# Turning batch 1's attention output with TensorE instead of DMA transposes, in a sliding-window attention and hard-swish kernel

## The chip, the cores and the metric

The kernel runs on one core of one Trainium2 chip. The metric is the device time of one execution in microseconds (us). Before the change three runs gave 332.79, 333.71 and 334.29 us, so the median is 333.71 us. The execution that was profiled took 332.83 us, and its span, which the times in the views below count from, is 331.1 us.

## What is computed

Two stages follow each other. The first is causal attention with a window of 64 keys, for 8 batches of 8 heads, 576 tokens each, head size 64. The second is an up-projection, a hard-swish and a down-projection over all 8 * 576 = 4608 tokens of width 512.

```python
scores = scale * np.matmul(q, k.transpose(0, 1, 3, 2))
rel = pos[:, None] - pos[None, :]
scores = np.where((rel >= 0) & (rel < 64), scores, -1e9)
attn = softmax(scores)                       # over the keys
x = np.matmul(attn, v).transpose(0, 2, 1, 3).reshape(4608, 512)
h = x @ w_in                                 # 512 -> 2048
out = (h * np.clip(h + 3, 0, 6) / 6) @ w_out # 2048 -> 512
```

## The kernel before, in words

**Pairs and blocks.** Attention goes by pairs of heads: pair `t` is batch `t // 4`, heads `2g` and `2g + 1` with `g = t % 4`. So batch 1 is the pairs 4 to 7, and batch 2 begins with pair 8. The second stage goes by blocks of 512 tokens. It reads `xT`, the attention output with the 512 features on the partitions (four groups of 128, one for each `g`) and tokens along the row. Block 1 is tokens 512 to 1023: the end of batch 0 and most of batch 1. Its first matmuls can start only when the columns of batch 1 are in `xT`, group by group.

**Work of a pair.** `turn` (L267) turns its queries and keys with 36 small TensorE transposes into two PSUM tiles (`tk`, `tq`), `turned` (L280) copies them to SBUF, `s_first` and `s_rest` (L289, L299) make the scores, `weights` (L314) the masked exponentials. `pv` (L381) multiplies these by V: 48 small matmuls (L396) whose sums, with the row sums in extra columns, fill two PSUM banks, the tile `o`. `pv_out` (L401) runs on VectorE: one row-sum reduction (L405), a reciprocal (L407), and three multiplies that normalise and write `opg0` (the first 64 tokens, L410) and `opl` (the other 512, two instructions at L415) to SBUF. `opg0` and `opl` have two buffers each, so pair `t + 2` writes where pair `t` wrote.

**Two ways into `xT`.** `x_` (L422) issues DMA transposes from the SP queue (L429): for batch 1, one for `opl` and one for `opg0` of each pair. `x_turned` (L440) turns the same data with five TensorE transposes (L444, L446) into a PSUM tile `xp`, which ScalarE copies to `xT` (L450). Before the change pairs 4 and 5 go by `x_` and pairs 6 and 7 by `x_turned`.

**PSUM.** There are eight banks: `ps_o` has one buffer of two banks (the tile `o`, and now and then half of it for a second-stage tile), `ps_t` three single banks, `ps_h` two single banks (the tiles `tk` and `tq` of `turn`, and some second-stage tiles), `ps_acc` one (the down-projection's sums `acc`).

**Order.** The instructions of each engine run in the order of the program, and that is written out by hand. The second stage lies in a queue `moe` of units; `weave(n)` emits the next `n` of them. In the stretch around the change these are the down-projection units of block 0, each four matmuls of 512 columns (L503). Each four units end with a copy on ScalarE (L509) and a store from the SP queue (L511). Ten of the sixteen have been emitted when pair 4 begins its `pv`. After pair 7 come `turn_two(8)` (the turn and copies of pair 8), the rest of the units, `shift(2)` (two SP DMAs at L156 and L157 that copy V of batch 2 within SBUF to a second alignment, after the loads of that V), and `begin(1, ...)` (L536): the up-projections of block 1 (L475) for groups 0 to 2 of three tiles, then `x_turned(7)`, then a fourth tile, then group 3 of all four. From there `group` (L709) runs pair after pair with units of the second stage between them. The POOL queue holds the loads: q and k of batch 2, V of batch 2, q and k of batch 3 are issued before this stretch (L118, L136), V of batch 3 after it.

```python
    for t in range(n, n + 4):              # L765, n = 4: batch 1
        pv(t)
        pv_out(t)
        if t < n + 2:
            x_(t)
        weave(2 if t == n else 1)
    turn_two(2 * NG)
    x_turned(n + 2)
    weave(len(moe))
    shift(2)
    queue_block(1)
    begin(1, (ps_t, ps_t, ps_acc, ps_o), lambda: x_turned(n + 3))
```

## Time and profile before

| | |
|---|---|
| median of the runs (lowest to highest) | 333.71 us (332.79 to 334.29) |
| the profiled execution | 332.83 us, span 331.1 us |
| mean granted TensorE clock | 0.985 of full speed |
| TensorE matmul busy | 304.5 us, 92% of the span |
| TensorE weight loads busy | 155.4 us, 47% |
| ScalarE busy | 186.2 us, 56% |
| VectorE busy | 177.1 us, 53% |
| GpSimd (POOL) busy | 114.7 us, 35% |
| DMA transposes at L429 | 30 of `opl`, 26 of `opg0`; median 2.9 and 3.2 us from issue to landing |

In the views PE is TensorE's matmuls, PEld its weight loads, DVE VectorE, ACT ScalarE, POOL GpSimd, SP the engine that issues stores and DMA transposes. A line of a timeline gives the start, the time until its last instruction ends, the engine, the source line, the tile written and those read, the number of instructions and, in brackets, the engine's idle time before it and what ended that. Matmuls overlap, so the spacing of two starts says what a piece of work costs and the duration of one does not. The profile has the tile `opg0` under the name `opg` and the fourth up-projection tile under `hTo`.

### The profile page before, as it was taken

The page shows a single profiled execution, that of the slowest core. Times are in us where ns is not written, and L with a number is a line of the kernel's source. Part 1 is how long each engine was busy: PE and PEld are TensorE (multiplying, and loading weights), DVE is VectorE, ACT ScalarE, POOL GpSimd, SP SyncE. Part 2 cuts the span into 40 slices and gives each one's busy share as a digit, 9 for nine tenths or more (in the row PEclk, how much of TensorE's full clock was granted, in tenths as well). Part 3 has the DMA queues.
Part 4 walks back from the last instruction along what each step waited for, and adds up shares of the span by engine and source line. Part 5 has one row for each costly group of instructions (what it writes and reads, how often), then busy time and mean ns, then how long its engine had stood idle before and what let it go on. Part 6 is the DMA issues. An engine that isn't in the chain of part 4 may idle for free.

```text
span 331.1 us, 11063 instructions
## 1 busy us (share of the span) xinstructions
PE 304.5 (92%) x4769; PEld 155.4 (47%) x4812; DVE 177.1 (53%) x382; ACT 186.2 (56%) x347; POOL 114.7 (35%) x149
## 2 busy tenths in 40 slices
PE   6879978198999999999999999999999999999992
PEld 3643444144555555555555555555544444444440
DVE  8676655128845673666366636663665354434300
ACT  2857673049857674677467736773685255554320
POOL 8952340007665633563356335633333000000000
PEclk9999999789999999999999999999999999999998
DMA  7999999932744965596559546954111200011011
GB/s 96 163 210 207 205 205 212 189 100 22 93 132 92 177 74 146 96 162 80 147 106 150 90 138 115 170 79 122 52 52 52 81 2 32 32 40 58 33 66 69
DMA packets 58680, 35.97 MB, mean 109 GB/s; under 512 B 40960, under 2 KB 52736, under 8 KB 58624
## 3 DMA queue, kind: packets, MB, share of 16 engines
q0 software_dynamic: 35712, 18.81, 42.6%
q1 hardware_dynamic: 22912, 16.38, 19.3%
q8 instruction: 39, 0.64, 0.8%
q14 instruction: 17, 0.14, 0.1%
HBM read 37.62 MB, written 9.44 MB: 142 GB/s over the span
## 4 chain that ended last, share of the span: by engine, by line
PE 78%; issue 10%; POOL 5%; DVE 3%; DMA 2%; ACT 1%; POOLq 0%; DVEq 0%; ACTq 0%
PE acc L503 35%; PE hT L475 33%; PE o L396 4%; PE s L308 2%; PE tk L274 2%; DMA V<-in_v_dram 2%; POOL qk L107 1%; POOL Pz L329 1%; POOL V L126 1%; DVE gT L484 1%; PE tq L274 1%; DVE opg L362 1%; POOL V L136 1%; ACT xT L376 0%; POOL P L326 0%
## 5 line engine op out<-in xcount | busy, mean ns | idle before, releaser
L484 DVE SCALAR_TENSOR_TENSOR gT<-t,hT 128x512 bf16<-128x512 bf16 x142 | 96.9, 687 | 84.2 <-ACT t L483 83.6
L503 PE MATMUL acc<-wout,gT 128*128 128x512 bf16 x547 | 134.4, 381 | 3.3 <-issue 1.9
L475 PE MATMUL hT<-xT,win 128*128 128x512 bf16 x555 | 135.1, 379 | 2.3 <-DVE gT L484 1.0
L483 ACT ACTIVATE t<-hT,half_const 128x512 bf16<-128x512 f32 x142 | 96.9, 688 | 52.1 <-PE hT L475 50.4
L475 PEld LDWEIGHTS <-win 128*128 128x128 bf16 x576 | 55.3, 98 | 67.3 <-issue 3.0
L503 PEld LDWEIGHTS <-gT 128*128 128x128 bf16 x576 | 54.8, 98 | 64.4 <-issue 1.2
L326 POOL TENSOR_TENSOR P<-e,first 64x256 bf16<-64x256 bf16 x24 | 15.9, 662 | 115.3 <-ACT e L317 113.4
L329 POOL TENSOR_TENSOR Pz<-e,band 128x512 bf16<-128x512 bf16 x48 | 54.1, 1145 | 0.0
L509 ACT COPY osb<-acc 128x512 f32<-128x512 f32 x36 | 21.1, 587 | 44.5 <-PE acc L503 38.8
L321 ACT ACTIVATE e<-s 128x512 bf16<-128x512 f32 x56 | 30.1, 592 | 0.9 <-PE s L308 0.9
L281 ACT COPY QZ<-tq 128x576 bf16<-128x576 bf16 x28 | 17.8, 637 | 14.9 <-PE tq L274 14.9
L396 PE MATMUL o<-V,Pz 64*64 64x65 bf16 x1120 | 16.7, 196 | 7.5 <-DVE opl L415 7.3
L136 POOL DMA_DIRECT2D V<-in_v_dram x22 | 17.9, 817 | 16.3 <-DMA win<-in_moe_w_in_dram 6.0
L396 PEld LDWEIGHTS <-Pz 64*64 64x64 bf16 x1120 | 13.5, 109 | 19.4 <-issue 9.1
L281 DVE COPY KT<-tk 128x576 bf16<-128x576 bf16 x28 | 20.8, 743 | 2.8 <-ACT e L317 1.9
L415 DVE TENSOR_TENSOR opl<-o,recs 128x256 bf16<-128x256 f32 x56 | 20.6, 406 | 0.0
L405 DVE TENSOR_REDUCE sums<-o 128x12 f32<-128x24 f32 x28 | 5.0, 179 | 29.0 <-PE o L396 29.0
L308 PE MATMUL s<-QZ,KT 64*64 64x64 bf16 x896 | 14.7, 195 | 1.8 <-issue 1.4
L317 ACT ACTIVATE e<-tk 64x128 bf16<-64x128 f32 x28 | 7.6, 270 | 13.4 <-PE tq L294 13.4
L274 PE MATMUL tk<-ident,qk 64*64 64x64 bf16 x504 | 14.1, 197 | 0.0
L274 PE MATMUL tq<-ident,qk 64*64 64x64 bf16 x504 | 14.1, 197 | 0.0
L410 DVE TENSOR_TENSOR opg<-o,recs 64x128 bf16<-64x128 f32 x28 | 7.9, 283 | 10.0 <-DMA xT<-opg 9.1
(92 smaller groups left out, 185.1 us busy)
## 6 DMA issues: line engine op xcount, KB each, us to landing
out_dram<-osb SPq DMA_DIRECT2D x36, 256.0 KB, 2.2
V<-in_v_dram POOLq DMA_DIRECT2D x16, 256.0 KB, 6.3
qk<-in_k_dram POOLq DMA_DIRECT2D x6, 576.0 KB, 5.9
qk<-in_q_dram POOLq DMA_DIRECT2D x6, 576.0 KB, 9.2
V<-V SPq DMA_DIRECT2D x6, 432.0 KB, 3.9
wout<-in_moe_w_out_dram POOLq DMA_DIRECT2D x2, 1024.0 KB, 18.0
win<-in_moe_w_in_dram POOLq DMA_DIRECT2D x2, 512.0 KB, 8.4
win<-in_moe_w_in_dram POOLq DMA_DIRECT2D x1, 1024.0 KB, 13.5
```

The costliest lines, as they stand in the source:

```text
L136: nc.gpsimd.dma_start(out=to[:, :, VO : VO + P], in_=v[b, :, m : m + n, :].rearrange("h (p r) d -> p h (r d)", r=2),)
L274: nc.tensor.transpose(out=hosts[t][z][halves[h], r * W : (r + 1) * W], in_=staged[b][halves[z], 2 * g + h, r * D : (r + 1) * D], identity= ...
L281: (nc.scalar.copy if z else nc.vector.tensor_copy)(out=(QZ[t % 4][:, 0] if z else KT[t % 4][:, W:]).rearrange("q (p r) -> q p r", r=RL), i ...
L308: nc.tensor.matmul(ss[h][halves[i], c, m, r], lhsT=keys(t, h, W * (w - 1), r), rhs=QZ[t % 4][halves[h], 0, w * W : (w + 1) * W], start=Tru ...
L321: nc.scalar.activation(out=e[:].rearrange("p c m r w -> p (c m r w)"), in_=ss[h][:].rearrange("p c m r w -> p (c m r w)"), func=EXP, scale ...
L329: muls[h].tensor_tensor(out=Pw[t % 4][:, h].rearrange("p c m r w -> p (c m) (r w)"), in0=e[:].rearrange("p c m r w -> p (c m) (r w)"), in1 ...
L396: nc.tensor.matmul(o[halves[c], i, c0 : c0 + D + 1], lhsT=p, rhs=vt[:, 2 * g + h, v0 : v0 + D + 1], start=(r == 0), stop=(r == 1), skip_gr ...
L475: nc.tensor.matmul(hT, lhsT=win16[:, g, fc * P : (fc + 1) * P], rhs=xT[:, g, t0 : t0 + TB], start=(g == 0), stop=(g == NG - 1),)
L483: nc.scalar.activation(out=t1[:], in_=hT, func=RELU, bias=half_const[:], scale=1.0 / 6.0)
L484: nc.vector.scalar_tensor_tensor(out=gT[:, fc, :], in0=t1[:], scalar=1.0, in1=hT, op0=MIN, op1=MULT)
L503: nc.tensor.matmul(acc[:], lhsT=gT[:, fc, ts * P : (ts + 1) * P], rhs=wout16[:, fc, :], start=(fc == 0), stop=(fc == NFC - 1),)
L509: nc.scalar.copy(out=osb[:], in_=acc[:])
```

## The change

Four things change, all in the stretch of batch 1. (1) Pairs 4 and 5 go by `x_turned` too, so four DMA transposes go and ten TensorE transposes and two ScalarE copies come. (2) The sums of pairs 4 and 6 go to two single banks of `ps_h`; those of 5 and 7 stay in the double bank of `ps_o`. For pairs 4 and 6 the row-sum reduction becomes two instructions, one for each bank. (3) `x_turned(t - 1)` is called after `pv` and `pv_out` of pair `t`, and one unit of the second stage follows for pairs 4, 5 and 6; the last three units come after `turn_two(8)`. (4) `shift(2)` moves ahead of these last three units.

```diff
-    def pv(t):
+    def pv(t, apart=False):
         b, g = divmod(t, NG)
-        o = ps_o.tile([P, 2, 512], F32, name="o", tag="o")
-        os_[t] = o
+        if apart:
+            o = [ps_h.tile([P, 512], F32, name="ot", tag="bk") for _ in range(2)]
+            os_[t] = [x[:].unsqueeze(1) for x in o]
+        else:
+            both = ps_o.tile([P, 2, 512], F32, name="o", tag="o")
+            o = [both[:, i] for i in range(2)]
+            os_[t] = [both[:]]
...
     def pv_out(t):
...
-        nc.vector.reduce_sum(out=sums[:], in_=ov[:, :, :, 0 : OC : OC - 1], axis=mybir.AxisListType.X)
+        for i, o in enumerate(ov):
+            nc.vector.reduce_sum(
+                out=sums[:] if len(ov) == 1 else sums[:, i : i + 1], in_=o[:, :, :, 0 : OC : OC - 1],
+                axis=mybir.AxisListType.X,
+            )
...
     for t in range(n, n + 4):
-        pv(t)
+        pv(t, t % 2 == 0)
         pv_out(t)
-        if t < n + 2:
-            x_(t)
-        weave(2 if t == n else 1)
+        if t > n:
+            x_turned(t - 1)
+        if t < n + 3:
+            weave(1)
     turn_two(2 * NG)
-    x_turned(n + 2)
+    shift(2)
     weave(len(moe))
-    shift(2)
     queue_block(1)
     begin(1, (ps_t, ps_t, ps_acc, ps_o), lambda: x_turned(n + 3))
```

More of the change, by code (lines that the diff above doesn't have):

```diff
@@ L396, in pv @@
                         nc.tensor.matmul(
-                            o[halves[c], i, c0 : c0 + D + 1], lhsT=p, rhs=vt[:, 2 * g + h, v0 : v0 + D + 1],
+                            o[i][halves[c], c0 : c0 + D + 1], lhsT=p, rhs=vt[:, 2 * g + h, v0 : v0 + D + 1],
                             start=(r == 0), stop=(r == 1), skip_group_check=True,
@@ L401, in pv_out @@
     def pv_out(t):
-        o = os_.pop(t)
-        ov = o[:, :, 0 : 6 * OC].rearrange("p i (s c) -> p i s c", c=OC)
+        ov = [o[:, :, 0 : 6 * OC].rearrange("p i (s c) -> p i s c", c=OC) for o in os_.pop(t)]
         sums = work.tile([P, 2, 6], F32, name="sums")
-        nc.vector.reduce_sum(out=sums[:], in_=ov[:, :, :, 0 : OC : OC - 1], axis=mybir.AxisListType.X)
+        for i, o in enumerate(ov):
[3 more added lines that the diff above has]
+            )
+        ov = [o[:, i] for o in ov for i in range(2 // len(ov))]
         rec = recs[:, t]
@@ L410, in pv_out @@
         nc.vector.tensor_tensor(
-            out=opg0[:], in0=ov[0:D, 0, 0:2, 1 : D + 1],
+            out=opg0[:], in0=ov[0][0:D, 0:2, 1 : D + 1],
             in1=rec[0:D, 0, 0:2].unsqueeze(2).to_broadcast([D, 2, D]), op=MULT,
@@ L415, in pv_out @@
             nc.vector.tensor_tensor(
-                out=opg[:, :, i], in0=ov[:, i, 2:6, 1 : D + 1].rearrange("p (m h) d -> p m h d", h=2),
+                out=opg[:, :, i], in0=ov[i][:, 2:6, 1 : D + 1].rearrange("p (m h) d -> p m h d", h=2),
                 in1=rec[:, i, 2:6].rearrange("p (m h) -> p m h", h=2).unsqueeze(3).to_broadcast([P, 2, 2, D]),
```

## The prediction, as it was put on record

> **What bounds the kernel now.** I read the page's 40 slices first: TensorE is at 9 tenths almost everywhere, so the kernel is bound by TensorE, except where the digit falls. The lowest one is the eighth slice, 58 to 66 us, and the granted clock falls there too.

> ```profile
> PE   6879978198999999999999999999999999999992
> PEclk9999999789999999999999999999999999999998
> ```

> Next the busy time by stretch. The columns are the stretch, its length, busy us (and instructions) of five engines, granted clock, DMA share, GB/s. From 58 to 65 us no engine works, while the DMA engines are full (a share over 1); the work after it, until 69.7, runs at a clock of 0.59.

> ```profile
> 50.00:58.00 8.00, 6.97 (x199) 3.51 (x200) 4.29 (x16) 2.19 (x6) 0.00 (x0) 1.00 1.45 213
> 58.00:65.00 7.00, 0.09 (x5) 0.02 (x4) 0.95 (x3) 0.00 (x0) 0.00 (x0) 0.79 1.25 198
> 65.00:69.70 4.70, 4.37 (x96) 2.67 (x98) 0.98 (x5) 1.28 (x2) 0.00 (x0) 0.59 0.30 48
> 69.70:74.00 4.30, 4.17 (x25) 1.74 (x27) 1.04 (x3) 1.80 (x3) 0.00 (x0) 1.00 0.52 170
> ```

> The waits from 50 to 70 us say who waited for whom (total, times, longest):

> ```profile
> DVE opg L410 <- DMA xT<-opg: 9.1, 2, 6.4
> PEld L396 <- DVE opl L415: 8.3, 2, 7.4
> PE o L396 <- DVE opl L415: 7.3, 2, 6.9
> ```

> VectorE's timeline gives the place. Pair 6 has its reciprocal at 57.38 but may write `opg0` only at 63.98, because pair 4's DMA transpose, issued at 55.24, still reads that buffer; pair 7 waits in the same way for pair 5's until 69.14.

> ```profile
> 57.38 0.23 DVE L407 RECIPROCAL recs<-sums 128x12 f32<-128x12 f32 x1
> 63.98 0.28 DVE L410 TENSOR_TENSOR opg<-o,recs 64x128 bf16<-64x128 f32 x1 [6.37 <-DMA xT<-opg]
> 64.19 0.74 DVE L415 TENSOR_TENSOR opl<-o,recs 128x256 bf16<-128x256 f32 x2
> ...
> 69.14 0.28 DVE L410 TENSOR_TENSOR opg<-o,recs 64x128 bf16<-64x128 f32 x1 [2.77 <-DMA xT<-opg]
> ```

> TensorE's timeline shows the chain: pair 7's `pv` needs the only `o`, which pair 6's VectorE work holds, and block 1's up-projection starts at 69.72, just behind the last transposes.

> ```profile
> 64.98 0.66 PE L396 MATMUL o<-V,Pz 64*64 64x65 bf16 x32 [6.91 <-DVE opl L415]
> ...
> 69.72 2.10 PE L475 MATMUL hT<-xT,win 128*128 128x512 bf16 x8
> ```

> The DMA view explains why a transpose takes so long here: in this stretch it lands 9.3 us (`opl`) and 9.7 us (`opg0`) after its issue, over the whole run 2.9 and 3.2. The loads of batches 2 and 3 fill the engines; a 256 KB store issued at 56.5 took 10.7.

> ```profile
> xT<-opl SPq DMA_TRANSPOSE x2, 9.3
> xT<-opg SPq DMA_TRANSPOSE x2, 9.7
> ```

> The chain that ended last is no help here: it follows POOL, which merely waits from 48.69 to 76.18, and calls that "issue".

> **The sum.** TensorE's work between pair 4's `pv` (51.74) and block 1's first matmul (69.72) can be priced by spacings of starts at full clock. One `pv`: 51.74 to 52.48, 54.40 to 55.14, 56.52 to 57.26, each 0.74. One unit of four matmuls: 52.48 to 54.40 for two, so 0.96. One `x_turned`: 71.75 to 72.12, 0.37. One `turn`: 46.14 to 46.45, 0.31.

> Before: 4 pv (2.96), 6 units (5.76), 1 `x_turned` (0.37), 1 turn (0.31), together 9.40 of the 17.98 us. The other 8.58 are the wait of 6.91, the half clock (from 64.98 to 69.72, 4.74 us for one pv, two units, one turn, one `x_turned`, 3.34: 1.40 more), and about 0.3 of small waits.

> After: the same and two more `x_turned`, 10.14. If nothing waits, block 1 starts at 51.74 + 10.14 = 61.88 in place of 69.72: **7.84 us earlier**.

> **Does anything wait?** I walk the new order on TensorE. Pair 4's two `ps_h` banks were last read by pair 7's exponentials, done at 51.03: free. pv 4 to 52.48, unit to 53.44, pv 5 (in `o`, free) to 54.18. `x_turned(4)` needs pair 4's `opl`. VectorE began that work at 52.43 and ended at 53.85; now a second reduction comes first. No row has a reduction of 12 elements: an extra of nothing (two halves of the 0.18 for 24) up to 0.23 (the reciprocal on 12); I take 0.21, the spacing from the reduction to the reciprocal, its nearest row. So 54.06, 0.12 before TensorE comes: the tightest place, at worst a tenth or two. Then `x_turned(4)` to 54.55, unit to 55.51, pv 6 to 56.25 (its banks free since 54.06). Pair 5's VectorE work, 1.42 us from 54.2, ends at 55.6; `x_turned(5)` at 56.25 to 56.62. The next unit begins a new `acc` and needs ScalarE's copy of the last one: unit done 55.5, copy 0.59, about 56.3. Unit to 57.58, pv 7 to 58.32 (`o` free since 55.6), `x_turned(6)` (pair 6 done by 57.9) to 58.69. `turn(8)` needs q of batch 2: issued 39.87, landed 15.9 later, 55.8, and pair 6's banks, 57.9: to 59.0. Three units to 61.88. Pair 6 writes `opg0` at about 56.7, long after `x_turned(4)` has read the buffer at 54.55. The two added ScalarE copies (0.64 each) lie in its idle 13.3 us between 55.1 and 68.4; what then ends latest for block 1 is TensorE itself. Without that cover 1.28.

> `shift(2)` leaves SP earlier. It waits there for V of batch 2 (the last load issued 44.24, 17.5 to land: 61.8), with only pair 7's old store and block 0's last store queued behind it. Its landing in full DMA traffic isn't shown: between 3.9 (the same copy at 71.2, in quiet) and 21.2 (the q load, the slowest of the stretch), nearest the transposes and the store, 8.6 to 10.7, on the same SP queue. At 10.7 it lands at 72.5; pair 8's `pv`, at 79.40 now and 71.56 then, would wait 0.9. But four transposes less run before it, and the loads end at 69.2, so I take no wait and keep 0.9 in the range.

> Behind block 1's start all order is as before: TensorE is busy 14.70 of 16 us from 74 to 90, 19.68 of 20 after. The only transfer on a fixed date is q of batch 3 (issued 48.01, 21.2 to land: 69.2); its first reader is at 90.10, then 82.3. So the gain should last to the end: 332.83 - 7.84 = 325.0 for the profiled execution, which lies 0.88 below the median; for the median **333.71 - 7.84 = 325.9**.

> [...] The clock is 1.00 in the row 50 to 58, where five units, 4.8 of 8 us, stand between three pairs' `pv`, and 1.00 from 40 to 52, with three turns. The new stretch from 51.74 to 59.0 has three units, 2.9 of 7.3 us, so less of the large matmuls, but no idle time; I count full clock. [...]

> **Rivals.**
> - *TensorE waits for its instructions, or the clock drops.* About 530 of its instructions now run in 10 us under full DMA traffic. Its longest wait on "issue" from 44 to 58 was 1.41 (the scores at 48.15). One or two such: 327.3 to 328.7. A clock stretch as long as before (7.0 * 0.21 + 4.7 * 0.41 = 3.4 us of clock lost in the two rows) costs at most 3.4: 329.3.
> - *A later load gives the time back.* If q and k of batch 3 land over 13 us later because of the earlier `shift`, pair 12's turn waits; 21 us later and nothing is left: 333.7. The loads have only 7 us left when `shift` begins.
> - *The `shift` becomes the wait (slower).* TensorE is in order, so all stands behind pair 8's `pv`. `shift` at 61.8 must land by 79.40, within 17.6 us, or the kernel is slower than before. At 21.2 it lands at 83.0, 3.6 late: 337.3. For it: it now starts in traffic in which the q load took that long. Against: the store of the same queue took 10.7, the slowest `shift` seen later 6.9.
> - *It doesn't do what it says.* If pair 6's wait were for the loads themselves, it would stay. But 55.24 + 8.6 is 63.84, and VectorE goes at 63.98.

> **How the numbers follow.** Forecast 0.78: 325.9. Instruction waits 0.08, the clock 0.04. A `shift` that costs about 1 us 0.04 (326.8). Time given back 0.02. Slower 0.04. The lower end is a run at the low edge (332.79, 0.9 below the median) and half gone of the 0.7 us for which the units waited on "issue" from 50 to 70: 324.6. The upper end is one wait of 1.41, the 0.9 of `shift`, 0.2 for the reduction and 0.6 for a run at the high edge: 329.0. That leaves out under 2 in 10. A measurement can tell about 0.5%, 1.7 us, from no change: faster 0.94, same 0.02, slower 0.04.

> **What would show it.** VectorE's work of pairs 4 to 7 back to back with no wait for a DMA; TensorE's idle of 6.91 gone and the clock 1.00 from 58 to 70; block 1's first L475 near 61.9; pair 8's `pv` near 71.6, released by POOL or nothing. Wrong would be: `x_turned(4)` or the turn of pair 8 late by over 0.5, "issue" over 1 us ahead of TensorE, or pair 8's `pv` released by the DMA of V.

## The result, and the profile after

The changed kernel takes 329.63 us (four runs, 328.73 to 331.38), the kernel before 333.45 us beside it (four runs, 332.79 to 334.29): a ratio of 0.989, 95% interval 0.9843 to 0.9938. A second comparison on another occasion gave 328.98 us and 0.9833 (0.9794 to 0.9872). So the change is faster by 3.8 to 4.9 us (1.1% to 1.7%; neither interval reaches 1), about half of the 7.84 us forecast. The time of 329.63 us lies above the range given, 324.6 to 329.0; that of the second comparison lies at its upper edge. The profiled execution took 329.89 us, its span is 328.2 us.

The slices of the profile's page first: the hole in the eighth slice is filled, but not to 9, and the clock still falls there.

```profile
PE   6989888799999999999999999999999999999992
PEclk9799999899999999999999999999999999999998
```

By stretch (columns as in the prediction): from 58 to 65 us TensorE works 5.08 of 7.00 us instead of 0.09, at a mean clock of 0.84, and the DMA engines are about as full as before (a share of 1.17, before 1.25).

```profile
50.00:58.00 8.00, 7.09 (x208) 3.86 (x207) 4.86 (x18) 3.84 (x9) 0.00 (x0) 1.00 1.44 213
58.00:65.00 7.00, 5.08 (x104) 2.57 (x102) 3.25 (x11) 1.82 (x3) 0.00 (x0) 0.84 1.17 253
65.00:69.70 4.70, 4.70 (x24) 2.02 (x23) 0.00 (x0) 0.87 (x2) 0.00 (x0) 0.88 0.29 82
```

In the waits from 50 to 70 us no engine waits for a DMA transpose, and TensorE's matmuls no longer wait for VectorE. What took their place has no engine's name:

```profile
PEld L401 <- issue: 4.7, 6, 2.0
...
PE o L401 <- issue: 2.8, 2, 1.9
```

TensorE's timeline shows where. L401 is now `pv`, L512 the units, L484 block 1's up-projection. Pair 5's `pv` stops after 3 matmuls, pair 7's after 17 (the rows show the runs between the stops; a few single rows between them are left out), and the last three units take 4.29 us up to block 1's start where 2.88 is their price at full clock.

```profile
54.23 0.22 PE L401 MATMUL o<-V,Pz 64*64 64x65 bf16 x3
55.36 0.44 PE L401 MATMUL o<-V,Pz 64*64 64x65 bf16 x29 [0.91 <-issue]
...
59.01 0.34 PE L401 MATMUL o<-V,Pz 64*64 64x65 bf16 x17
61.28 0.32 PE L401 MATMUL o<-V,Pz 64*64 64x65 bf16 x15 [1.92 <-issue]
...
62.52 4.45 PE L512 MATMUL acc<-wout,gT 128*128 128x512 bf16 x12
66.81 2.10 PE L484 MATMUL hT<-xT,win 128*128 128x512 bf16 x9
```

From pair 4's `pv` (52.75) to block 1's start (66.81) it is 14.06 us; before it was 17.98, the forecast was 10.14. The 3.92 us above the forecast are two stops (0.91 and 1.92), a clock of one half from 62.7 to 66.1 (1.41), and 0.32 saved elsewhere. Everything behind block 1's start takes what it took: 331.1 - 69.72 is 261.4, and 328.2 - 66.81 is 261.4. The stretch is entered 1.0 us later than in the profile before; over the profiles of this study pair 4's `pv` starts between 51.7 and 52.8, whatever the kernel. So the profiles differ by 2.9 us and the medians by 3.8.

### The profile page after: what moved, and what is told of

It reads as the page before. It is cut to its first block, busy times and chain, and to the rows that moved or that the text cites. A ratio compares the mean times of both kernels' runs of the same rounds, so it can differ in the third digit from the quotient of the medians.

```text
span 328.2 us, 11123 instructions
## 1 busy us (share of the span) xinstructions
PE 310.7 (95%) x4822; PEld 157.2 (48%) x4822; DVE 177.2 (54%) x384; ACT 187.6 (57%) x349; POOL 114.9 (35%) x149
## 4 chain that ended last, share of the span: by engine, by line
PE 75%; issue 8%; POOL 7%; DMA 7%; ACT 0%; POOLq 0%; ACTq 0%
PE acc L512 36%; PE hT L484 31%; DMA qk<-in_q_dram 7%; PE o L401 4%; PE s L308 2%; PE tk L274 2%; POOL qk L107 1%; POOL V L126 1%; POOL Pz L329 1%; PE tq L274 1%; POOL win L162 1%; POOL qk L118 1%; POOL wout L168 1%; POOL V L136 1%; POOL band L194 0%
## 5 line engine op out<-in xcount | busy, mean ns | idle before, releaser
L512 PE MATMUL acc<-wout,gT 128*128 128x512 bf16 x576 | 139.6, 383 | 0.0
L484 PE MATMUL hT<-xT,win 128*128 128x512 bf16 x568 | 136.0, 379 | 1.6 <-DVE gT L493 1.0
L484 PEld LDWEIGHTS <-win 128*128 128x128 bf16 x576 | 55.3, 98 | 67.2 <-issue 3.2
L512 PEld LDWEIGHTS <-gT 128*128 128x128 bf16 x576 | 55.1, 99 | 64.8 <-issue 2.2
L326 POOL TENSOR_TENSOR P<-e,first 64x256 bf16<-64x256 bf16 x24 | 15.9, 665 | 111.6 <-ACT e L317 109.7
L329 POOL TENSOR_TENSOR Pz<-e,band 128x512 bf16<-128x512 bf16 x48 | 54.2, 1147 | 0.0
L518 ACT COPY osb<-acc 128x512 f32<-128x512 f32 x36 | 21.2, 588 | 45.7 <-PE acc L512 42.8
L401 PEld LDWEIGHTS <-Pz 64*64 64x64 bf16 x1120 | 13.4, 108 | 15.3 <-issue 13.2
L410 DVE TENSOR_REDUCE sums<-o 128x12 f32<-128x24 f32 x26 | 4.6, 178 | 29.7 <-PE o L401 29.7
L424 DVE TENSOR_TENSOR opl<-o,recs 128x256 bf16<-128x256 f32 x52 | 19.2, 406 | 0.0
L401 PE MATMUL o<-V,Pz 64*64 64x65 bf16 x1040 | 15.7, 195 | 3.1 <-issue 2.8
L274 PEld LDWEIGHTS <-qk 64*64 64x64 bf16 x1008 | 11.5, 105 | 3.2 <-issue 2.1
```

The costliest lines, as they stand in the source:

```text
L274: nc.tensor.transpose(out=hosts[t][z][halves[h], r * W : (r + 1) * W], in_=staged[b][halves[z], 2 * g + h, r * D : (r + 1) * D], identity= ...
L329: muls[h].tensor_tensor(out=Pw[t % 4][:, h].rearrange("p c m r w -> p (c m) (r w)"), in0=e[:].rearrange("p c m r w -> p (c m) (r w)"), in1 ...
L401: nc.tensor.matmul(o[i][halves[c], c0 : c0 + D + 1], lhsT=p, rhs=vt[:, 2 * g + h, v0 : v0 + D + 1], start=(r == 0), stop=(r == 1), skip_gr ...
L484: nc.tensor.matmul(hT, lhsT=win16[:, g, fc * P : (fc + 1) * P], rhs=xT[:, g, t0 : t0 + TB], start=(g == 0), stop=(g == NG - 1),)
L512: nc.tensor.matmul(acc[:], lhsT=gT[:, fc, ts * P : (ts + 1) * P], rhs=wout16[:, fc, :], start=(fc == 0), stop=(fc == NFC - 1),)
L518: nc.scalar.copy(out=osb[:], in_=acc[:])
```

## What the two stops are

A stop in the middle of one `pv`, after 3 equal matmuls, does not look like a wait for data. The counts tell more. Here are two stretches, from the end of one stop to the end of the next (first number behind the length: TensorE's matmuls, in brackets their count; then the weight loads):

```profile
49.10:55.30 6.20, 5.29 (x128) 2.60 (x128) 3.31 (x11) 3.02 (x7) 0.23 (x1) 1.00 1.34 222
55.30:61.25 5.95, 4.00 (x128) 2.41 (x128) 2.77 (x11) 1.86 (x3) 0.00 (x0) 1.00 1.40 210
```

128 matmuls and 128 weight loads are 256 instructions, both times. The profile lists a DMA queue for instructions (q8) that moved 39 packets, 0.64 MB: 16.4 KB each, which comes to 64 bytes for each of 256 instructions. That this queue is TensorE's is inferred: its 4822 matmuls and 4822 weight loads are 37.7 times 256. So I formed **theory 1**: TensorE's instructions arrive in pages of 256 (from here on "page" alone means such a block of instructions); the packet of the next page starts late while the loads fill the DMA engines, and TensorE stops at the end of its page. One packet falls between two stops, and it starts 3.6 to 3.7 us after the page before it was begun (begun 49.16, packet 52.87, on at 55.36; begun 55.36, packet 58.94, on at 61.28): 6.20 and 5.92 us for a page, with 5.29 and 4.00 us of TensorE's work in it. For the pages begun from 71 to 105 us, where the mean DMA share is 0.48 in place of 1.34 and 1.40, the packet starts 0.7 to 1.0 us after. The two stops cost 2.83 us together.

The kernel before had it too. Its stop of 1.41 us at 48.15 stood in its profile, and the next wait on issue, 0.63 us before a weight load at 54.07, comes exactly 128 weight loads later (two matmul records are missing):

```profile
48.10:54.05 5.95, 5.47 (x126) 2.78 (x128) 3.25 (x10) 3.02 (x7) 0.59 (x1) 1.00 1.26 225
```

The rivals were **theory 2**, that many small matmuls outrun the supply whatever the traffic, and that these stops are some unnamed wait that belongs to these matmuls.

## The experiments

Each was compared with the kernel before in the same session. Times are medians; "the change" is the changed kernel.

| run | us | before | ratio (95% interval) |
|---|---|---|---|
| e1 change, loads held | 326.11 | 334.12 | 0.9781 (0.9743 to 0.982) |
| e2 before, loads held | 329.38 | 334.12 | 0.9876 (0.9838 to 0.9914) |
| e3 change, units in the loop | 326.19 | 334.12 | 0.9771 (0.9736 to 0.9805) |
| e4 change, one double bank | 329.18 | 334.12 | 0.9862 (0.983 to 0.9894) |
| a2 the change again | 328.98 | 333.90 | 0.9833 (0.9794 to 0.9872) |
| e5 change, pages moved | 328.83 | 333.90 | 0.9846 (0.9812 to 0.988) |
| e7 e1 and e3 together | 324.79 | 333.90 | 0.973 (0.9696 to 0.9764) |
| e8 e7, V of batch 2 held too | 324.78 | 333.90 | 0.9723 (0.969 to 0.9755) |
| e6 change, shift back | 329.41 | 333.38 | 0.9872 (0.9837 to 0.9907) |
| e9 before, only `x_turned` | 327.86 | 333.38 | 0.9815 (0.9777 to 0.9853) |
| e10 e7 with a spare load | 326.06 | 333.38 | 0.9767 (0.9729 to 0.9806) |

**The loads held back (e1).**

```diff
+    held = consts.tile([D, 1], BF16, name="held")
+    nc.gpsimd.tensor_copy(out=held[:], in_=opgs[n + 3][1][:, 0, 0:1])
+    staged[3] = load_qk(3)
     turn_two(2 * NG)
...
-    staged[3] = load_qk(3)
     group(2 * NG - 1, 4)
```

> The changed kernel, but the loads of q and k of batch 3 are held back on POOL until pair 7's opg0 is written (about 59 to 62 us, not 48). Theory 1 (TensorE runs out of instructions: they come in pages of 256, and under full DMA traffic the next page is ready only about 6 us after the last one was begun): with the loads of batch 3 gone from the stretch, the stall of 1.92 us in pair 7's pv goes, the stall of 0.91 in pair 5's pv may shrink, and the half clock from 62.7 to 66.1 (1.4 us lost) goes with the idle time: about 3.3 us faster than the change, 326.3 us. Theory 2 (the page comes late because the stretch has so many small matmuls, whatever the DMA engines do): the stalls stay, 329.6 us.

326.11 us. Pair 7's stop shrinks from 1.92 to 0.28, at the same matmul. No packet of q8 starts from 57 to 60 us, where the change has one at 58.94; the page was begun at 54.81, so its packet started at most 2.2 us after instead of 3.6. Pair 5's stop stays (0.91); of the loads those of batch 2 still run then, at a DMA share of 1.34 from 50 to 58 us. The clock stays at 1.00 from 50 to 69.7 us.

```profile
54.81 0.44 PE L401 MATMUL o<-V,Pz 64*64 64x65 bf16 x29 [0.91 <-issue]
...
58.47 0.34 PE L401 MATMUL o<-V,Pz 64*64 64x65 bf16 x17
59.09 0.32 PE L401 MATMUL o<-V,Pz 64*64 64x65 bf16 x15 [0.28 <-issue]
```

The same TensorE instructions, the same page, less traffic (a DMA share of 1.22 over that page instead of 1.40, and 0.73 instead of 1.17 from 58 to 65 us): theory 2 falls.

**The same in the kernel before (e2).** The edit is that of e1, in the kernel before.

> The kernel before with nothing but the same hold of batch 3's q and k loads. If the DMA transposes were slow because the loads filled the DMA engines: they land about 3 us after their issue, pair 6 goes on at about 58.4 in place of 63.98, block 1 begins about 6 us earlier: 327.4 us. If four transposes on one queue are slow by themselves: landings stay at 8 to 10 us and the time at 333.4 us.

329.38 us: the mechanism holds, but 4.7 us were gained where about 6 were expected. In its DMA view from 50 to 66 us the transposes land after 5.9 and 3.6 us instead of 9.3 and 9.7, but pair 4's is issued at 54.59 while the loads of batch 2 still run (a DMA share of 1.62 from 50 to 58 us), so pair 6 goes on at 60.74, not at 58.4.

```profile
60.74 0.28 DVE L410 TENSOR_TENSOR opg<-o,recs 64x128 bf16<-64x128 f32 x1 [2.43 <-DMA xT<-opg]
```

```profile
xT<-opl SPq DMA_TRANSPOSE x2, 5.9
xT<-opg SPq DMA_TRANSPOSE x2, 3.6
```

Moving one pair of loads gave the kernel before as much as the whole change did (ratio 0.9876 against 0.989 and 0.9833).

**The units moved into the loop (e3).**

```diff
         if t < n + 3:
-            weave(1)
+            weave(2 if t < n + 2 else 1)
```

> The changed kernel with two of the late units of the down-projection moved into the loop (two after pair 4, two after pair 5, one after pair 6, one at the end): the same instructions, more large matmuls in each page of 256. Theory 1: the second page is then begun at about 55.2 where it is ready at 55.3 (stall 0.1 in place of 0.91), the third is reached about 60.0 and ready at 61.2 (stall 1.2 in place of 1.92): 1.5 us faster than the change, 328.1 us, and 326.7 if the clock stays up. Rival (TensorE waits for data, so that order within the stretch does not matter): 329.6 us.

326.19 us, a little under the better of the two figures. A page now holds more large matmuls, so its work lasts longer (5.13 us from 54.36 to the next stop; 4.00 in the change): the stop in pair 5's `pv` is gone (0.41 us before a unit in its place, where 0.1 was expected), the other comes after 9 matmuls of pair 7's `pv` with 1.34 us, and the clock stays at 1.00 from 50 to 69.7 us.

```profile
54.36 0.39 PE L512 MATMUL acc<-wout,gT 128*128 128x512 bf16 x1 [0.41 <-issue]
...
60.83 0.38 PE L401 MATMUL o<-V,Pz 64*64 64x65 bf16 x23 [1.34 <-issue]
```

**One double bank for all pairs (e4).** `pv(t, t % 2 == 0)` becomes `pv(t)`.

> The changed kernel without the alternation: all four pairs' sums in the double bank of ps_o. Theory 1: the waits for VectorE that come back (pair 5's pv until 55.0, pair 6's by 0.25, pair 7's by 0.5 us) lie where TensorE waits for its page anyway, so at most 0.3 us slower than the change, 329.6 to 329.9 us. Rival (the alternation carries part of the gain): pairs 5, 6 and 7 wait 0.7, 0.25 and 0.5 us on top, 331.1 us.

329.18 us, no slower than the change. TensorE waits for `opl` three times, 1.0 us in all; the stop in pair 5's `pv` shrinks from 0.91 to 0.22 in return, and pair 7's is 1.90. The new banks save these waits, and in the change the page takes most of that back.

**The pages moved against the code (e5, beside a2).** Sixteen small matmuls more at the start, whose results are not used:

```diff
     warm(ps_h, 12)
+    wt = ps_h.tile([P, TB], F32, name="wt", tag="bk")
+    for _ in range(16):
+        nc.tensor.matmul(wt[:, 0:16], lhsT=zeros[:, 0:P], rhs=zeros[:, 0:16], start=True, stop=True)
```

> The changed kernel itself, for a comparison on the same chip: 329.6 us, with TensorE waiting on issue in pair 5's pv after 3 matmuls and in pair 7's after 17.

> The changed kernel with 16 small matmuls (of 16 columns) more at the start, where TensorE waits for the first loads. Theory 1 (pages of 256 instructions): every stall on issue comes 32 instructions, 16 pairs of weight load and matmul, earlier in the program: the one after 7 scores of pair 6 moves to after 31 transposes of pair 7's turn, the one after 3 matmuls of pair 5's pv to after 39 of pair 4's, the one after 17 of pair 7's pv to after 1. The time stays within 1 us of the change. Rival (the stalls belong to these matmuls, by a wait that the profile does not name): the stalls stay after 7, 3 and 17.

a2 stopped where the change did (0.64 and 2.2 us). In e5 every stop moved by 16 pairs: into the turn of pair 7 with 5 transposes left of 36, into pair 4's `pv` with 9 matmuls left of 48, and to pair 7's `pv` after 1.

```profile
48.14 0.21 PE L274 MATMUL tq<-ident,qk 64*64 64x64 bf16 x1 [1.47 <-issue]
...
54.34 0.21 PE L401 MATMUL ot<-V,Pz 64*64 64x65 bf16 x1 [1.93 <-issue]
...
59.19 0.21 PE L401 MATMUL o<-V,Pz 64*64 64x65 bf16 x1
60.53 0.45 PE L401 MATMUL o<-V,Pz 64*64 64x65 bf16 x31 [1.13 <-issue]
```

These stops belong to a place in the instruction stream, not to any work: 32 instructions more ahead of them put all three 32 instructions earlier in the program, still 256 apart. The time is that of a2.

**Both cures together (e7), and V held too (e8).** e7 has the edits of e1 and e3. e8 also calls `load_v(2)` only after pair 4's `pv_out`, behind a copy of its `opg0` on POOL.

> The changed kernel with both: batch 3's loads of q and k held back, and the units moved into the loop (2, 2, 1, then 1). Theory 1: the stall in pair 5's pv goes to 0.1 by the units, the one in pair 7's to nothing by the loads; only the one before the stretch stays: 325.2 us. If the two edits mend the same thing: 326.1 us, as each alone.

> As the one with both, and the loads of V of batch 2 held back until pair 4's opg0 is written. Theory 1: the DMA engines then have only batch 2's q and k before 53 us, so the stall of 1.2 to 1.5 us in pair 6's scores shrinks too: 324.2 us. Against it: V of batch 2 now lands at about 60 and shift after it at about 65, before pair 8's pv at about 71; if it lands later than that, pair 8 waits and the time is above 325.2.

e7 takes 324.79 us: neither `pv` stops, and from 58 to 65 us TensorE works 6.77 of 7.00 us.

```profile
58.00:65.00 7.00, 6.77 (x149) 3.74 (x140) 3.44 (x12) 3.03 (x5) 1.54 (x3) 1.00 0.63 127
```

By ratio to the kernel before it is the best version together with e8, and both beat the change; the intervals overlap with those of e1 and e3. e8's expectation failed: 324.78 us, nothing more. The stop in pair 6's scores did not shrink (1.67 us, 1.36 in e7). e8 does not hold q of batch 2, which in the profile before loads from 39.87 to 55.8 us; that this load kept the stop was not tested.

**The shift back (e6).** `shift(2)` stands behind the last units again.

> The changed kernel with shift(2) back behind the last units. Theory 1 (the loads of batch 3 hold up the pages; shift begins when the third page is nearly there): same as the change, 329.0 us within 0.5. Rival (the earlier shift adds the traffic that delays the page): the stall of 1.9 to 2.2 us in pair 7's pv shrinks by about a half, 328 us.

329.41 us; pair 7's stop was 2.47, and the clock fell: the last three units took 3.24 us (2.60 in e1, at 1.00), and the execution's mean clock is 0.984 (0.995 in e1). The earlier `shift` costs nothing and brings nothing here.

**Only the transposes (e9).** In the kernel before, `x_(t)` becomes `x_turned(t)`, nothing else.

> The kernel before with one line changed: x_turned in place of x_ for pairs 4 and 5, right behind their pv_out, without new banks, new order or earlier shift. TensorE then waits for VectorE twice (about 1.4 us each, at 52.5 and 57), and reaches the pages of 256 so much later that they are there. Theory 1: about 4.9 us gained of the wait of 6.91 and the half clock, 329.0 us, the same as the whole change, because what the banks and the order save is waited for again at the page. Rival (banks and order carry their share of the gain): 3 us slower than the change, 332 us.

327.86 us, 1.1 faster than expected and, by ratio to the kernel before, level with the change (0.9815 against 0.989 and 0.9833; the intervals overlap). The other three parts of the change together thus gained nothing that was measured. TensorE waits for VectorE, but not once for a page in this stretch, and its clock stays at 1.00:

```profile
PE xp L444 <- DVE opg L410: 1.8, 2, 0.9
PE o L396 <- DVE opl L415: 0.6, 1, 0.6
```

**The load put back as a spare (e10).** e7, and behind V of batch 2 a load of the same size into a tile that nobody reads:

```diff
+    spare = consts.tile([P, H, RL * D], BF16, name="spare")
+    for z, src in enumerate((k, q)):
+        nc.gpsimd.dma_start(out=spare[halves[z]], in_=src[3].rearrange("h (p r) d -> p h (r d)", r=RL))
```

> The kernel with the held loads and the moved units (324.8 us), plus a load of batch 3's q and k into a spare tile that nobody reads, queued behind V of batch 2 as the held loads were in the change. Theory 1 (traffic delays the pages): the stall in pair 7's pv comes back with 1.1 to 1.6 us as in the kernel with the units alone: 326.2 us. Rival (what helped was something else about the held loads: their buffer, POOL's order): 324.8 us.

326.06 us: the stop is back, after the same matmul as in e3, if shorter (0.79 us; 1.1 to 1.6 was expected).

```profile
61.01 0.38 PE L401 MATMUL o<-V,Pz 64*64 64x65 bf16 x23 [0.79 <-issue]
```

e10 keeps e7's buffer and its order on POOL and only adds loads. So it is the traffic.

## Why the prediction was wrong, point by point

- **What bounds the kernel before: right.** VectorE's work of the four pairs has no wait for a DMA left, and e9 shows that this alone is worth 5.5 us (333.38 to 327.86).
- **Why the transposes were slow: right.** With the loads held (e2) they land after 3.6 and 5.9 us.
- **The prices of the pieces: right.** Without stops and half clock the stretch takes 9.82 us against 10.14. The second reduction costs less than the 0.21 taken: two take 0.24 in all against 0.18 for one.
- **"Does anything wait?": the step that failed.** The walk gave TensorE every instruction the moment its data was there. 534 instructions in 10 us need two new pages, and in that traffic a page took 6.20 and 5.92 us. The prediction knew the wait of 1.41 on "issue", but gave it a chance of 0.08, as a mishap that might come once or twice. It was on a schedule that could be counted in the trace of before: 128 weight loads from one to the next. The two pages cost 0.91 and 1.92.
- **The clock: wrong, as a consequence.** It fell to one half for 3.4 us behind the longer stop in the change (62.7 to 66.1), which cost 1.41. In a2 its mean from 58 to 65 us was 0.80, and in e6 the last three units took 3.24 us in place of 2.60. It didn't fall in e5: behind its stop of 1.93 the unit's last three matmuls took 0.74 us up to the next `pv`, as in a2 (54.78 to 55.52, 53.25 to 53.99), and behind that of 1.13 the clock is 1.00 from 58 to 74 us. Nor did it fall in e4, with a stop of 1.90 at nearly the same time as the change's, nor in e2, with a wait of 2.97 (both 1.00 from 50 to 69.7 us). So the length of a stop does not settle it, and no run was made to find what does. The six runs of a2, one kernel, have mean clocks from 0.986 to 0.995, and the two shortest (327.71 and 326.94 us) the highest: what the clock costs differs from one execution to the next. The added transposes alone do not cost it: e1, e3 and e7 run them at 1.00 (e1 and e3 from 50 to 69.7 us, e7 from 58 to 65).
- **The shift, q of batch 3, the end: right.** TensorE has no new wait there; the gain at block 1's start reaches the end in full.
- The rival "instruction waits or the clock" gave 327.3 to 328.7 for the one and 329.3 for the other, with chances of 0.08 and 0.04. Both came together, and the measured 329.63 lies above either.

## What to carry to other kernels

When a long wait is removed, ask what the engine's next few hundred instructions need besides data: where small matmuls run dense beside heavy loads, TensorE may be limited by the arrival of its instructions, as here, where a page with 4.00 us of work took 5.92 us at a DMA share of 1.40. Look for waits on "issue" in the middle of equal instructions and count the instructions between two of them, weight loads included. If they are the same count apart each time (128 weight loads and 128 matmuls here), thin the loads in that stretch (e1, 326.11 us) or mix in large matmuls, so that each page holds more time (e3, 326.19 us); here the reordering that only tightened the small work gained nothing.
